# Seven of sixteen filter and matrix loads in the filter stage, and a z written contiguously

## The chip, the core and the metric

The kernel runs on one core of a Trainium2 chip. That core has a matrix engine (TensorE, in the profile PE, with its weight loads as PEld), a vector engine (VectorE, DVE), a scalar engine (ScalarE, ACT), GpSimd (POOL), which here does little more than issue transfers, and SyncE (SP), which only issues them. All transfers are carried by the core's 16 DMA engines, whoever issues them. The metric is the device time of one execution in microseconds.

## The reference

Two identical layers are applied to `x` of 2048 tokens by 576 features. Each layer adds a spectral block and then an MLP block to `x`:

```python
x = x + _A_ref(_layernorm(x), A_w_r, A_w_i)                   # spectral
x = x + _B_ref(_layernorm(x), B_w1, B_b1, B_w2, B_b2)         # MLP
# _A_ref: X = rfft2(x) over tokens and features; X = X * (w_r + 1j*w_i); irfft2, as bf16
# _B_ref: h = gelu(layernorm(x) @ w1 + b1), w1 is 576 x 4608;  h @ w2 + b2
```

The filter `w_r`, `w_i` has 2048 x 289 elements each. Inputs and output are bf16.

## The kernel before

The tokens are held in SBUF as 16 tiles of 128 x 576. The Fourier transforms are matrix products with constant matrices. The transform over the 2048 tokens is split into two factors, 16 and 128, with an exchange of partitions between them. So a layer goes through four stages.

**The filter stage** (`SpectralIn`, here meaning the forward transform up to the exchange) takes one tile after another. `fold` makes sum and difference of a tile's halves, `turn` transposes them on PE and copies the result out with ACT (`xT`), and `dft_d` multiplies by the feature-transform matrix into two PSUM banks: even frequencies (o = 0) in one bank, odd ones (o = 1) in the other. Each bank holds a real and an imaginary half (r) of 145 float32 values (j). At L423, one ACT instruction scales the 580 values by the tile's inverse deviation and writes them as bf16 to `z`, where the frequencies lie in natural order, so that even and odd alternate. `dft_v` multiplies by the 16-point matrix, and ACT or DVE copies the result to `y1`. `exchange` (L479) lets SP issue one transfer per tile that spreads it over 8 partitions of `vx`. In layer 0 the tiles come in one loop (`run_all`). In layer 1 they are worked in between the steps of layer 0's MLP, and only the last tile is on its own.

**The middle stage** (`middle`) needs all of `vx`. In a loop of 20 steps, step i does `dft_u(i)` on PE (matrix `c_f2`), an ACT copy, `weigh(i)` on DVE (products with the filter tiles `wks`), `join(i-1)` on DVE, and `idft_c(i-4)` on PE (matrix `i1s`) with a copy and another `exchange`, into `hx`. The slot numbers 0 to 15 go through four groups j = 0 to 3 of four slots each. Group j uses `f2` j, `wr` j, `wi` j and `i1` j, which makes sixteen loads in all, each 289 or 384 KB. Twelve filler matmuls (`keep_busy`) stand ahead of the loop.

**The back stage** (`SpectralOut`) needs all of `hx`, and 16 filler matmuls stand ahead of it. It adds the result to `x` and prepares the MLP's first input. Its matrices are `c_r1` and `c_gd`.

**The MLP** goes through four blocks of four tiles. `mlp_up` makes the hidden values of a block (GELU on ACT), and `mlp_down` the output, tile by tile. In layer 0, `fold_twice` and `turn_dma` prepare layer 1's spectral input as the tiles come out, and a second form of `dft_d` with the constant `c_fd2` transforms them. The w2 weights come in four parts during the first `mlp_up`, one for each of its first four groups of hidden chunks.

**The order of the work** is written by hand: every engine executes its instructions in program order. The loads that matter here go through `load` (L216), which puts the transfer on POOL's queue and, with an argument `behind`, lets POOL wait first for a marked instruction. In the filter stage, the list `first` (L882 to L892) is spread over the steps of `run_all`, each entry behind a tile's `xT` or `y1` copy. In the middle stage, `mid_loads` names for slot n the loads that wait for `join(n)`. In the MLP, the n-th entry of `w2_loads` waits for a GELU of group n.

Of the kernel before, what the change touches and what calls it, by code (L numbers as in the profile page):

```python
# [18 lines left out]
P = 128  # L19
# [3 lines left out]
KP = 2 * KH  # L23
# [100 lines left out]
def kernel(  # L124
# [15 lines left out]
    def const_ap(key):  # L140
        return nc.inline_tensor(hc[key], name=f"const_{key}").ap()
# [15 lines left out]
    def big_ps(shape, dtype=F32):  # L157
        return ps_big.tile(shape, dtype, tag="big", name=f"psb{uid()}")

    def sm_ps(shape, dtype=BF16):  # L160
        return ps_sm.tile(shape, dtype, tag="sm", name=f"pss{uid()}")
# [8 lines left out]
    def at(buf, shape, off=0):  # L170
        n = int(np.prod(shape[1:]))
        dims = "abcd"[: len(shape) - 1]
        return buf[0 : shape[0], off : off + n].rearrange(f"p ({' '.join(dims)}) -> p {' '.join(dims)}", **dict(zip(dims[1:], shape[2:])))
# [4 lines left out]
    c_fd2 = persist.tile([P, 4 * KH + 2 * KP], BF16, name="c_fd2")  # L178
    c_k1 = persist.tile([P, 3, P], BF16, name="c_k1")
    c_f2 = persist.tile([P, 16, 3, P], BF16, name="c_f2")  # L180
    c_r1 = persist.tile([P, 2, 256], BF16, name="c_r1")
    c_gd = persist.tile([P, 6, DH], BF16, name="c_gd")
# [3 lines left out]
    b1_rows = persist.tile([NFC, 128], BF16, name="b1_rows")  # L186
    b2_bc = persist.tile([P, D], BF16, name="b2_bc")
# [28 lines left out]
    def load(out, in_, behind=None):  # L216
        ins = nc.gpsimd.dma_start(out=out, in_=in_).ins
        if behind is not None:
            tc.add_manual_dep(ins, marks[behind].name, SYNC, reason="pace of the loads")
# [12 lines left out]
    def load_w(j, ri, behind=None):  # L232
        wv = (A_w_r, A_w_i)[ri].rearrange("(c e) k -> c e k", e=16)
        load(wks[j][:, :, ri, 0 : KP - 1], wv[:, j::4, :], behind)

    def load_i1(j, behind=None):
        load(i1s[j][:], i1_ap[:, j::4], behind)

    def load_f2(j, behind=None):
        load(c_f2[:, j::4], f2_ap[:, j::4], behind)  # L240

    def load_w1(ci, h):
        cols = slice(h * F_FF // 4, (h + 1) * F_FF // 4)
        return nc.sync.dma_start(out=w1_sb[:, ci, cols], in_=B_w1[ci * 128 : (ci + 1) * 128, cols]).ins

    def load_w1r(h):
        rest = B_w1[512:576, :].rearrange("d (j two p) -> d two j p", two=2, p=128)
        return nc.sync.dma_start(out=w1r_sb[64 * h : 64 * h + 64], in_=rest[:, h]).ins
# [4 lines left out]
    def place_w2():  # L253
        r_sb = shared_tile(BF16)
        w2_parts[:] = at(v_sb, [P, 8, D]), at(v_sb, [P, 8, D], 8 * D), at(r_sb, [P, 10, D]), at(r_sb, [P, 10, D], 10 * D)
# [5 lines left out]
    def load_w2(g, behind):  # L261
        rows = B_w2[w2_first[g] * 128 : w2_first[g + 1] * 128, :]
        load(w2_parts[g], rows.rearrange("(fc p) d -> p fc d", p=128), behind)
# [38 lines left out]
    class SpectralIn:  # L302
# [99 lines left out]
        def dft_d(self, t):  # L402
            pz = big_ps([P, 2, 512])
            if ("xT2", t) in self.st:
                xT = self.st.pop(("xT2", t))
                for o in range(2):
                    at_rest = 4 * KH + o * KP
                    nc.tensor.matmul(pz[:, o, 0:KP], lhsT=xT[:, 4, :], rhs=c_fd2[:, at_rest : at_rest + KP], start=True, stop=False)
                    for part in range(2):
                        g = FOLDS.index((o, part))  # L410
                        nc.tensor.matmul(
                            pz[:, o, part * KH : (part + 1) * KH], lhsT=xT[:, g, :], rhs=c_fd2[:, g * KH : (g + 1) * KH],
                            start=False, stop=(part == 1),
                        )
            else:
                xT = self.st.pop(("xT", t))
                for o in range(2):
                    for q, ci in enumerate(HALF_CHUNKS[o]):
                        nc.tensor.matmul(  # L419
                            pz[:, o, 0:KP], lhsT=xT[:, ci, :], rhs=c_fd[:, 3 * o + q, :], start=(q == 0), stop=(q == 2),  # L420
                        )
            z = work.tile([P, 2, KP], BF16, tag="z", bufs=3)
            nc.scalar.activation(  # L423
                out=z[:].rearrange("p r (j o) -> p r o j", o=2),
                in_=pz[:, :, 0:KP].rearrange("p o (r j) -> p r o j", r=2),
                func=ACT.Copy, scale=self.st.pop(("rs", t)),
            )
            self.st["z", t] = z
# [453 lines left out]
    first = [("x", 2), ("x", 3)]  # L882
# [1 line left out]
        first += [("f2", j), ("wr", j), ("wi", j), ("i1", j)]  # L884
    calls = {"x": load_x, "f2": load_f2, "i1": load_i1, "wr": lambda j, b: load_w(j, 0, b), "wi": lambda j, b: load_w(j, 1, b)}
    paced = {}
    for n, (kind, j) in enumerate(first[:-3]):
        i = 1 + 5 * n // 8
        if i <= NT:
            paced.setdefault(i, []).append(lambda kind=kind, j=j, i=i: calls[kind](j, ("turn", order[i - 1])))  # L890
        else:
            paced.setdefault(i, []).append(lambda kind=kind, j=j, i=i: calls[kind](j, ("y1", order[i - 4])))  # L892
# [6 lines left out]
    for li in range(N_LAYERS):  # L899
        last = li == N_LAYERS - 1  # L900
        out_loads = []
        mid_loads = {}
        if li == 0:
            mid_loads = {
                0: [lambda b: load_w(3, 0, b)],
                1: [lambda b: load_w(3, 1, b)],
                2: [lambda b: load_i1(3, b)],
                3: [lambda b: load(c_r1[:], const_ap("r1"), b)],
                4: [lambda b: load(c_gd[:], const_ap("gd"), b), lambda b: load(b1_rows[:], B_b1.rearrange("(fc p) -> fc p", p=128), b)],
                6: [lambda b: load(c_fd2[:], const_ap("fd2"), b)],  # L910
                5: [lambda b: load(b2_bc[:], B_b2.partition_broadcast(P), b)],
            }
        middle(vx, hx, wks, i1s, mid_loads)
        if li == 0:
            b1p = sm_ps([P, NFC])
            nc.tensor.transpose(b1p[:, :], b1_rows[:, :], ident[0:NFC, 0:NFC])
            nc.vector.tensor_copy(out=b1_sb[:], in_=b1p[:])
            out_loads = [lambda ci=ci: load_w1(ci, 0) for ci in range(4)] + [lambda h=h: load_w1r(h) for h in range(2)]
            out_loads += [lambda ci=ci, h=h: load_w1(ci, h) for h in range(1, 4) for ci in range(4)]
        prep = Prep(0, sqrt=True)  # L920
        SpectralOut(hx).run_all(prep, out_loads)
        place_w2()
        w2_loads = [lambda b, g=g: load_w2(g, b) for g in (0, 1, 2, 3)]
        if last:
            mlp(li, prep, None, w2_loads)
        else:
            vx, hx = at(b_sb, [P, 16, 2, KP]), at(v_sb, [P, 16, 2, KP])
            mlp(li, prep, SpectralIn(vx, sqrt=False), w2_loads)
            for j in range(4):
                b = ("y1", order[-1]) if j >= 2 else None  # L930
                load_w(j, 0, b)
                load_w(j, 1, b)
                load_i1(j, b)
# [27 lines left out]
```

## Time and profile before

| What | us |
|---|---|
| Median of 6 runs (747.42 to 751.56) | 747.67 |
| The profiled execution, its own time | 748.9 |
| Its span, first to last instruction | 747.1 |
| PE busy in the span | 725.4 |
| ACT busy | 314.8 |
| DVE busy | 273.0 |
| Layer 0: filter stage, to the middle's first matmul | 0 to 43.3 |
| Layer 0: middle stage, to the back stage's first matmul | 43.3 to 72.0 |
| Layer 1: middle stage, likewise | 405.4 to 432.5 |

The profile's page gives busy time per engine, the span in slices, the DMA queues, and the chain of work that ended last. Its further views list single instructions in order of time, waits by engine, and busy time in chosen stretches. In the latter, "DMA share" is the mean busy share of the 16 DMA engines and GB/s is what they moved. All times are counted from the start of the span.

### The profile page before, as it was taken

The numbers are of one execution on the slowest core, as the hardware profiler recorded it, in microseconds if no ns is written. First come the engines' busy times: TensorE is split into PE (matmuls) and PEld (weight loads), VectorE is DVE, ScalarE is ACT, GpSimd is POOL, SyncE is SP. The second block draws the span as 40 slices with busy tenths as digits, with TensorE's granted clock in tenths as the row PEclk, the third lists the DMA queues.
The fourth block names the chain that finished last, engine by engine and source line by source line (L and its number), as shares of the span: only waits on it lengthen the run. The fifth ranks groups of instructions, "written<-read, shape, count | busy, mean of one in ns | idle before, by whom it ended". The sixth has DMA issues, their size and how long they took to land. (4 is left out here: it accounts for less than half of the span.)

```text
span 747.1 us, 12382 instructions
## 1 busy us (share of the span) xinstructions
PE 725.4 (97%) x5000; PEld 454.7 (61%) x5038; DVE 273.0 (37%) x932; ACT 314.8 (42%) x530; POOL 61.6 (8%) x114
## 2 busy tenths in 40 slices
PE   7989999999999999999998999999999999999998
PEld 4655744784478447844785675467546744774476
DVE  6975870366036603630354859001400140010011
ACT  6955866115521452146324777530262045105600
POOL 4220012000100110000004000020100010000000
PEclk9999999999999999999999999999999999999999
DMA  8744925410121112210027401560001010200000
GB/s 261 233 127 148 283 66 181 120 44 26 44 56 50 26 44 54 52 35 0 18 44 223 126 17 36 171 150 25 35 11 44 17 44 0 45 17 8 1 17 17
DMA packets 49417, 54.45 MB, mean 73 GB/s; under 512 B 29892, under 2 KB 41104, under 8 KB 49360
## 3 DMA queue, kind: packets, MB, share of 16 engines
q1 hardware_dynamic: 41328, 23.99, 12.6%
q0 software_dynamic: 7600, 29.10, 12.3%
q8 instruction: 39, 0.64, 0.4%
q10 hardware_dynamic: 432, 0.58, 0.2%
q14 instruction: 18, 0.15, 0.1%
HBM read 29.34 MB, written 8.59 MB: 51 GB/s over the span
## 5 line engine op out<-in xcount | busy, mean ns | idle before, releaser
L806 PEld LDWEIGHTS <-h_sb 128*128 128x128 bf16 x2304 | 224.7, 98 | 58.8 <-issue 1.0
L761 PEld LDWEIGHTS <-w_sb 128*128 128x128 bf16 x1152 | 109.4, 98 | 142.5 <-issue 17.2
L274 DVE BATCH_NORM_STATS2 stats<-x_sb 128x6 f32<-128x288 bf16 x110 | 43.8, 440 | 1.1 <-DMA x_sb<-in_A_x_dram 1.1
L720 DVE TENSOR_SCALAR xn<-x_sb,mv,rs 128x576 bf16<-128x576 bf16 x24 | 9.4, 427 | 66.6 <-DMA quad_1769<-xn 27.6
L769 PEld LDWEIGHTS <-w1r_sb 64*128 64x128 bf16 x288 | 10.8, 94 | 24.5 <-issue 17.0
L802 DVE TENSOR_TENSOR xb<-x_sb,b_bc 128x576 f32<-128x576 bf16 x32 | 24.0, 749 | 0.0
L723 POOL COPY xn<-xn 128x64 bf16<-128x64 bf16 x24 | 6.4, 267 | 155.1 <-DVE xn L720 155.1
L527 PEld LDWEIGHTS <-h_sb 128*128 128x128 bf16 x128 | 12.1, 97 | 11.6 <-issue 6.2
L496 PEld LDWEIGHTS <-c_f_83 128*128 128x128 bf16 x128 | 12.3, 97 | 8.9 <-issue 3.3
L775 ACT ACTIVATE h_sb<-psb_5993,b_sb 128x512 bf16<-128x512 f32 x2 | 1.3, 684 | 37.9 <-PE psb_5993 L769 37.9
L775 ACT ACTIVATE h_sb<-psb_6591,b_sb 128x512 bf16<-128x512 f32 x2 | 1.3, 683 | 37.8 <-PE psb_6591 L769 37.8
L775 ACT ACTIVATE h_sb<-psb_7189,b_sb 128x512 bf16<-128x512 f32 x2 | 1.3, 683 | 37.8 <-PE psb_7189 L769 37.8
L829 DVE TENSOR_TENSOR x_sb<-psb_7429,xb 128x576 bf16<-128x576 f32 x1 | 0.8, 758 | 43.4 <-PE psb_7429 L806 43.4
L214 PEld LDWEIGHTS <-zeros 128*128 128x128 bf16 x95 | 9.4, 101 | 9.6 <-issue 1.7
L829 DVE TENSOR_TENSOR x_sb<-psb_4049,xb 128x576 bf16<-128x576 f32 x1 | 0.8, 758 | 39.5 <-PE psb_4049 L806 39.5
L352 DVE TENSOR_TENSOR xf<-ef 128x256 bf16<-128x256 f32 (+1 forms) x56 | 13.6, 305 | 0.5
L829 DVE TENSOR_TENSOR x_sb<-psb_6233,xb 128x576 bf16<-128x576 f32 x1 | 0.8, 759 | 33.6 <-PE psb_6233 L806 33.6
L829 DVE TENSOR_TENSOR x_sb<-psb_6831,xb 128x576 bf16<-128x576 f32 x1 | 0.8, 758 | 33.6 <-PE psb_6831 L806 33.6
L435 PEld LDWEIGHTS <-c_k_82 128*128 128x128 bf16 x120 | 11.3, 99 | 2.5
L419 PEld LDWEIGHTS <-xT 128*128 128x128 bf16 x96 | 9.9, 104 | 4.1 <-issue 1.1
L829 DVE TENSOR_TENSOR x_sb<-psb_3245,xb 128x576 bf16<-128x576 f32 x1 | 0.8, 758 | 28.7 <-PE psb_3245 L806 28.7
L678 ACT ACTIVATE h_sb<-x_sb 128x576 bf16<-128x576 bf16 x16 | 11.2, 699 | 0.1
(1367 smaller groups left out, 1500.1 us busy)
## 6 DMA issues: line engine op xcount, KB each, us to landing
w_sb<-in_B_w_dram SPq DMA_DIRECT2D x16, 288.0 KB
v_sb<-in_B_w_dram POOLq DMA_DIRECT2D x4, 1152.0 KB, 6.3
h_sb<-const_i POOLq DMA_DIRECT2D x8, 384.0 KB, 6.5
shared_1465<-in_B_w_dram POOLq DMA_DIRECT2D x2, 1440.0 KB, 7.7
shared_5390<-in_B_w_dram POOLq DMA_DIRECT2D x2, 1440.0 KB, 7.4
v_sb<-shared_113 SPq DMA_DIRECT2D x16, 145.0 KB
b_sb<-shared_691 SPq DMA_DIRECT2D x16, 145.0 KB
v_sb<-shared_4645 SPq DMA_DIRECT2D x16, 145.0 KB
```

What stands on the lines that cost most here:

```text
L214: nc.tensor.matmul(pw[:], lhsT=zeros[:], rhs=zeros[:, 0:1].to_broadcast([P, 512]), start=True, stop=True)
L274: nc.vector.bn_stats(out=stats[:, h, :], in_=x_sb[:, t, h * DH : (h + 1) * DH])
L352: nc.vector.tensor_tensor(out=xf[:, at0 : at0 + 2 * n].rearrange("p (g d) -> p g d", g=2), in0=ef[:, :, first : first + n], in1=ef[:, :, b ...
L419: nc.tensor.matmul(pz[:, o, 0:KP], lhsT=xT[:, ci, :], rhs=c_fd[:, 3 * o + q, :], start=(q == 0), stop=(q == 2),)
L435: nc.tensor.matmul(py[:, r, 0:KP], lhsT=c_k1[:, pl, :], rhs=z[:, ri], start=(q == 0), stop=(q == 1))
L496: nc.tensor.matmul(px[:, o, 0:KP], lhsT=c_f2[:, e, pl, :], rhs=vx[:, e, ri, :], start=(q == 0), stop=(q == 1))
L527: nc.tensor.matmul((ph, odd)[o][:, o, 0:KP], lhsT=i1[:, n % 4, pl, :], rhs=xp[:, ri, :], start=(q == 0), stop=(q == 1))
L678: nc.scalar.activation(out=at(h_sb, [P, D], 512 * 34), in_=x_sb[:, self.quad[i], :], func=(ACT.Copy, ACT.Square)[k], accum_out=self.s12[:, ...
L761: nc.tensor.matmul(acc[p][q], lhsT=w1_sb[:, ci, fc * 128 : (fc + 1) * 128], rhs=yT[:, ci, :], start=(first and ci == 0), stop=(not first a ...
L769: nc.tensor.matmul(acc[p][q], lhsT=w1r_sb[rows, p, :], rhs=yT[rows, 4, :], start=first, stop=not first)
L802: nc.vector.tensor_tensor(out=xb[:], in0=xr, in1=b2_bc[:].rearrange("p (h n) -> p h n", h=2), op=ALU.add)
L806: nc.tensor.matmul(po[:, h, 0:DH], lhsT=hts[fc][:, i * 128 : (i + 1) * 128], rhs=w2_chunk(fc)[:, h * DH : (h + 1) * DH], start=(fc == 0), ...
```

## The change

Three things change. First, the filter stage of layer 0 now issues the list `first` without its last seven entries, where it left out the last three. So `wr` 2, `wi` 2, `i1` 2 and `f2` 3 move into the middle stage, which then has seven of the sixteen loads, and its order is written anew. Second, `c_fd2` moves from the middle stage to a fifth entry of `w2_loads` in layer 0's MLP. Third, in `dft_d` the loop order of the ACT instruction is turned: for every j it handles both o, so that it writes `z` element after element and reads the two PSUM banks in turn, where it read each bank in runs of 145 and wrote every second element.

```diff
@@ dft_d @@
             nc.scalar.activation(
-                out=z[:].rearrange("p r (j o) -> p r o j", o=2),
-                in_=pz[:, :, 0:KP].rearrange("p o (r j) -> p r o j", r=2),
+                out=z[:].rearrange("p r (j o) -> p r j o", o=2),
+                in_=pz[:, :, 0:KP].rearrange("p o (r j) -> p r j o", r=2),
                 func=ACT.Copy, scale=self.st.pop(("rs", t)),
@@ paced loads of the filter stage @@
-    for n, (kind, j) in enumerate(first[:-3]):
+    for n, (kind, j) in enumerate(first[:-7]):
@@ loads of the middle stage, layer 0 @@
-                0: [lambda b: load_w(3, 0, b)],
-                1: [lambda b: load_w(3, 1, b)],
-                2: [lambda b: load_i1(3, b)],
-                3: [lambda b: load(c_r1[:], const_ap("r1"), b)],
-                4: [lambda b: load(c_gd[:], const_ap("gd"), b), lambda b: load(b1_rows[:], B_b1.rearrange("(fc p) -> fc p", p=128), b)],
-                6: [lambda b: load(c_fd2[:], const_ap("fd2"), b)],
-                5: [lambda b: load(b2_bc[:], B_b2.partition_broadcast(P), b)],
+                0: [lambda b: load_w(2, 0, b), lambda b: load_w(2, 1, b)],
+                1: [lambda b: load_f2(3, b)],
+                2: [lambda b: load_i1(2, b)],
+                3: [lambda b: load_w(3, 0, b), lambda b: load_w(3, 1, b)],
+                5: [lambda b: load_i1(3, b)],
+                6: [lambda b: load(c_r1[:], const_ap("r1"), b), lambda b: load(b1_rows[:], B_b1.rearrange("(fc p) -> fc p", p=128), b)],
+                7: [lambda b: load(c_gd[:], const_ap("gd"), b), lambda b: load(b2_bc[:], B_b2.partition_broadcast(P), b)],
@@ w2 loads @@
         w2_loads = [lambda b, g=g: load_w2(g, b) for g in (0, 1, 2, 3)]
+        if li == 0:
+            w2_loads.append(lambda b: load(c_fd2[:], const_ap("fd2"), b))
```

## The prediction

> **What bounds the kernel now.** I read the page first.
>
> ```profile
> span 747.1 us, 12382 instructions
> PE 725.4 (97%) x5000; PEld 454.7 (61%) x5038; DVE 273.0 (37%) x932; ACT 314.8 (42%) x530; POOL 61.6 (8%) x114
> ```
>
> PE is busy all along, but some of that is filler. The chain of work from 494 us on is MLP matmuls alone, so a delay in an earlier stage is not made good later. The change touches layer 0's filter stage (to 43.3) and middle stage (to 72.0). So next I read ACT's instructions in order of time:
>
> ```profile
> 23.32 0.92 ACT L423 ACTIVATE z<-psb_411,rs 128x580 bf16<-128x580 f32 x1
> 24.11 0.67 ACT L339 COPY xT<-pss_427 128x640 bf16<-128x640 bf16 x1
> 24.67 0.65 ACT L440 CAST shared_113<-psb_438 128x580 bf16<-128x580 f32 x1
> 25.20 0.94 ACT L423 ACTIVATE z<-psb_445,rs 128x580 bf16<-128x580 f32 x1
> 25.98 0.69 ACT L339 COPY xT<-pss_458 128x640 bf16<-128x640 bf16 x1
> 26.56 0.30 ACT L282 ACTIVATE sq<-mv_420,c_eps 128x2 f32<-128x2 f32 x1
> 27.16 0.93 ACT L423 ACTIVATE z<-psb_480,rs 128x580 bf16<-128x580 f32 x1 [0.30 <-PE psb_480 L419]
> 27.95 0.67 ACT L339 COPY xT<-pss_494 128x640 bf16<-128x640 bf16 x1
> ```
>
> Two tiles take 3.61 us (20.50 to 24.11) or 3.84 (24.11 to 27.95), 3.72 on average. From start to start a z costs 0.78, an xT 0.57, a y1 0.53, a root 0.30: 2 x 0.78 + 2 x 0.57 + 0.53 + 0.30 = 3.53 us for two tiles. ACT is the bound with 0.2 to spare. DVE is close behind: its shorter rounds, with no idle, take 3.6.
>
> For the middle stage I read busy time by stretches, and the waits of PE.
>
> ```profile
> core 0: us, PE busy (x) PEld busy (x) DVE busy (x) ACT busy (x) POOL busy (x), PEclk, DMA share, GB/s
> 49.00:59.00 10.00, 9.27 (x64) 6.08 (x64) 10.00 (x34) 8.80 (x16) 3.45 (x6) 1.00 0.82 233
> 59.00:69.00 10.00, 9.89 (x61) 5.77 (x61) 6.57 (x22) 5.18 (x9) 0.00 (x0) 1.00 0.54 183
> ```
> ```profile
> PE psb_705 L496 <- DMA v_sb<-shared_113: 1.4, 1, 1.4
> PE pss_1036 L567 <- DMA b_sb<-shared_691: 1.2, 1, 1.2
> ```
>
> The second wait is the one to look at: the back stage starts at 72.0 because the last exchange comes late, although filler covers PE until 70.8. SP issued it at 66.6, so it took 5.3 us. In layer 1, whose middle has hardly any loads, the same transfer is issued at 428.7 and all traffic is over by 432.0: 3.3 us, and PE never waits. So layer 0's exchanges are held up by the loads beside them, and the rows show how: after the loads, from 59 to 69, the traffic stays at a flat 183 GB/s and a share of 0.54, a backlog being worked off.
>
> [...]the trace has 920, while the plain copy of the same 580 values (642) and of 290 (401) agree with the slope.[...] No row of before reads PSUM element by element from two banks.
>
> **z, part by part.** Removed is the write at every second element. A GELU with one pointer, 512 values, takes 684: 257 fixed. With 257 + 580 x 0.833 = 740 as the best case, the gain is at most 180 ns. Added is a read that changes bank with every element[...]. If that costs a second cycle per element, z takes 257 + 580 x 1.667 = 1,224 ns, 300 more. I take this end: [...]already the milder stride on the write side goes with 180 ns lost.
>
> At 1,224, two tiles cost ACT 3.53 + 0.60 = 4.13, with a little dependency idle 4.2, against 3.72: +0.48. The loop has some 6.5 such pairs at full pace (15.7 to 36.2): +3.1. The first tiles and the last z, on the way to the final exchange, add 0.3 each: +3.7. At 740, ACT falls to 3.17 and DVE's 3.58 takes over: -0.14 x 6.5 - 0.16 = -1.0. The 15 z of the MLP cost nothing either way: ACT idles 5.8 us before most of them, and dft_v stands 24 matmuls (2.9 us) behind dft_d; without that cover they would cost 15 x 0.3 = 4.5.
>
> **Loads out of the filter stage.** 289 + 289 + 384 + 384 = 1,346 KB leave it. No compute instruction waits there for anything but x, so only the last exchange can gain: issued 39.7, waited for until 43.2, 3.5 us against 3.3 undisturbed: -0.2. POOL's issues (0.75 each) delay nobody.
>
> **Loads into the middle.** There 1,346 come and c_fd2's 290 goes: +1,056 KB.[...] The shares from 47 to 71 add up to 14.6 us of all engines. The 16 exchanges (16 x 145 KB = 2.38 MB) at 183 GB/s need 13.0 us on their engines, 7.0 of the whole set. That leaves 7.5 us per engine for the 1,965 KB loaded, 3.84 ns per KB. Check: 13.0 + 7.5 = 20.5 of the 21.5 us from 49 to 70.5: these engines hardly rest. Then 1,056 x 3.84 = +4.06 us until the last exchange lands: about 76.0 where it was 72.0. As PE already waits, all of it shows: +4.0.
>
> The moved loads also come later for their users. By the same price, and the pace of before (57% of the engine's time goes to loads: `i1` 3 landed 6.7 us after its issue at 49.4), `f2` 3 lands at 55.6 (needed 56.4), `i1` 2 at 58.1 (57.2), `wi` 3 at 61.8 (59.5), `i1` 3 at 64.3 (62.1). So PE or DVE stalls by some 2.3 us in all: DVE at weigh(12), with join and idft_c behind it. That moves the end of the filler from 70.8 to 73.1, still before 76.0, so it is contained in the 4.0 and not added. c_r1 and c_gd land by 68, before the back stage.
>
> **c_fd2 in the MLP.** POOL's fifth load waits for the GELU at 131.6, and behind it in POOL's queue stand the copies and stores for the next block's input, issued from 127.3 on. They start 5.5 us later; then DVE's fourth norm (135.1, behind which the first output tile's add at 142 waits) comes near 138 to 140. SP's transpose (138.3) moves to about 143; its result is wanted near 171. c_fd2 lands near 139, first used at 155.4. Cost 0; with that cover gone at most 5.5.
>
> **Sum.** +3.7 - 0.2 + 4.0 = +7.5. The profiled execution, 748.9 with its span of 747.1, would become 756.4; it lies 1.2 above the median, so 747.67 + 7.5 = 755.2.
>
> **Rivals.**
> (1) z gets faster (740 to 900 ns), loads as above: -1.0 - 0.2 + 4.0 = +2.8, 750.5.[...]
> (2) The loads hide: backlog is worked off in the middle's own time[...]. With slow z: +3.7 - 0.2 = +3.5, 751.2. Against it: the flat 0.54 until 69.
> (3) Not slower: z at 740 with loads hidden, -1.2, 746.5. Decisive is the last exchange's landing: if it comes before the filler's end at 70.8, the loads cost nothing, and PE even saves its 1.2 us wait: -2.4, 745.3.[...]
>
> **Chances and range.** Likeliest case 0.50; rival 1 0.28; rival 2 0.12; rival 3 0.10. Two executions of this kernel can't be told apart below 0.3%, 2.2 us. Rival 3 lies almost wholly inside that, a fifth of it beyond; a quarter of rival 1 falls inside and a little of rival 2: faster 0.02, same 0.18, slower 0.80. Range: below, rival 1 with loads at 3 us, 749.3; above, loads at 5.5[...] and z at 1,300: 758.5. The likeliest case alone: 753 to 758.
>
> **What would show it.** z's duration at L423 (1.2 or 0.74) and the distance between tiles in the filter stage (4.2 or 3.6 for two); PE's wait at L567 for the exchange growing from 1.2 towards 4, with DMA shares of 0.8 until some 66 us; a stall of DVE at L507 or L508, or PE at L527, for h_sb. The prediction is wrong if z stays near 0.92 or falls, or if L567 starts by 73 plus what the filter stage lost.

## The result and the profile after

| | before | changed |
|---|---|---|
| Median, us | 748.16 (20 runs, 746.63 to 751.56) | 751.24 (10 runs, 748.87 to 751.61) |
| Profiled execution, its own time / its span | 748.9 / 747.1 | 750.09 / 748.3 |
| Filter stage's end: the middle's first matmul (L496) | 43.27 | 42.24 |
| Back stage's first matmul (L567) | 71.99 | 73.02 |
| Length of the middle, between these two | 28.72 | 30.78 |
| From L567 to the first MLP's first matmul (L761) | 25.43 | 25.44 |

The changed kernel is slower by the ratio 1.0032 (95% interval 1.0020 to 1.0045), some 3 us. The forecast was 755.2; the change costs less than half of what was summed. (After the change nine of the sixteen filter and matrix loads stand in the filter stage and seven in the middle, not the other way round, as the title could be read.) The page after, first its span and part 1, busy time by engine:

```profile
span 748.3 us, 12381 instructions
PE 724.9 (97%) x5000; PEld 454.5 (61%) x5038; DVE 273.2 (37%) x932; ACT 310.5 (41%) x530; POOL 61.6 (8%) x114
```

ACT has lost 4.3 us of busy time, DVE and PE next to nothing. So `z` has become cheaper, where the forecast had made it dearer. ACT in order of time in the changed kernel, columns start, duration, engine, line, and in brackets the idle time before and what ended it:

```profile
26.23 0.74 ACT L423 ACTIVATE z<-psb_476,rs 128x580 bf16<-128x580 f32 x1 [0.30 <-PE psb_476 L419]
26.87 0.68 ACT L339 COPY xT<-pss_490 128x640 bf16<-128x640 bf16 x1
27.44 0.66 ACT L440 CAST shared_113<-psb_501 128x580 bf16<-128x580 f32 x1
27.98 0.77 ACT L423 ACTIVATE z<-psb_508,rs 128x580 bf16<-128x580 f32 x1
...
30.47 0.69 ACT L339 COPY xT<-pss_557 128x640 bf16<-128x640 bf16 x1
```

A `z` takes 0.74 to 0.77 us instead of 0.92. Two tiles take 3.60 us (26.87 to 30.47), and ACT now has idle time of its own, 0.30 ahead of every second `z`. DVE has none in these rounds, and its work on two tiles starts again after 3.60 us:

```profile
26.70 0.81 DVE L274 BATCH_NORM_STATS2 stats<-x_sb 128x6 f32<-128x288 bf16 x2
...
30.30 0.81 DVE L274 BATCH_NORM_STATS2 stats<-x_sb 128x6 f32<-128x288 bf16 x2
```

It is the new bound, at the 3.6 that the prediction's best case had for it. The middle starts 1.03 us earlier.

Then the loads. Busy time by stretches in the changed kernel, the last two columns being the DMA share and GB/s:

```profile
core 0: us, PE busy (x) PEld busy (x) DVE busy (x) ACT busy (x) POOL busy (x), PEclk, DMA share, GB/s
49.00:59.00 10.00, 9.22 (x64) 6.12 (x64) 10.00 (x33) 8.80 (x16) 4.46 (x8) 1.00 0.98 280
59.00:69.00 10.00, 8.35 (x53) 4.79 (x52) 5.63 (x19) 4.25 (x8) 0.00 (x0) 1.00 0.54 189
69.00:71.00 2.00, 2.00 (x11) 0.88 (x9) 0.00 (x0) 0.00 (x0) 0.00 (x0) 1.00 0.51 175
71.00:73.00 2.00, 0.34 (x2) 0.01 (x1) 0.00 (x0) 0.00 (x0) 0.00 (x0) 1.00 0.09 31
```

Where before had a share of 0.82 from 49 to 59, it is 0.98 now. The flat tail at 0.54, exchanges alone (8.6 of the 16 DMA engines), lasts until 70.5 and not until 69. The waits in the same stretch (in total, times, longest):

```profile
ACT shared_687 L535 <- DMA b_sb<-shared_687: 2.5, 3, 1.7
...
PE pss_1035 L567 <- DMA b_sb<-shared_687: 1.7, 1, 1.7
PE psb_975 L527 <- DVE shared_687 L514: 1.6, 1, 1.6
DVE shared_687 L533 <- DMA b_sb<-shared_687: 1.5, 1, 1.5
```

The second line is the wait that the forecast followed, 1.69 us where it was 1.22. The first and the last are new, and the forecast has nothing of them: the copies into the eight `h` buffers (L528, slot n mod 8) wait for the exchange that last read from the same buffer. The third, PE's wait at L527, follows from them: `join` (L514) stands behind DVE's wait in DVE's order. None of these waits is for a load.

### The profile page after: what moved, and what is told of

Read it like the earlier page. It is cut to its first block, busy times and chain, and to the rows that moved or that the text cites. A ratio compares the mean times of both kernels' runs of the same rounds, so it can differ in the third digit from the quotient of the medians.

```text
span 748.3 us, 12381 instructions
## 1 busy us (share of the span) xinstructions
PE 724.9 (97%) x5000; PEld 454.5 (61%) x5038; DVE 273.2 (37%) x932; ACT 310.5 (41%) x530; POOL 61.6 (8%) x114
## 5 line engine op out<-in xcount | busy, mean ns | idle before, releaser
L761 PEld LDWEIGHTS <-w_sb 128*128 128x128 bf16 x1152 | 109.4, 98 | 142.4 <-issue 17.2
L527 PEld LDWEIGHTS <-h_sb 128*128 128x128 bf16 x128 | 12.1, 97 | 13.2 <-issue 7.8
L496 PEld LDWEIGHTS <-c_f_83 128*128 128x128 bf16 x128 | 12.3, 97 | 9.2 <-issue 3.6
L829 DVE TENSOR_TENSOR x_sb<-psb_7429,xb 128x576 bf16<-128x576 f32 x1 | 0.8, 758 | 43.4 <-PE psb_7429 L806 43.4
L829 DVE TENSOR_TENSOR x_sb<-psb_4049,xb 128x576 bf16<-128x576 f32 x1 | 0.8, 758 | 39.5 <-PE psb_4049 L806 39.5
L829 DVE TENSOR_TENSOR x_sb<-psb_6831,xb 128x576 bf16<-128x576 f32 x1 | 0.8, 759 | 33.6 <-PE psb_6831 L806 33.6
L829 DVE TENSOR_TENSOR x_sb<-psb_6233,xb 128x576 bf16<-128x576 f32 x1 | 0.8, 758 | 33.6 <-PE psb_6233 L806 33.6
L829 DVE TENSOR_TENSOR x_sb<-psb_3245,xb 128x576 bf16<-128x576 f32 x1 | 0.8, 759 | 28.7 <-PE psb_3245 L806 28.7
```

What stands on the lines that cost most here:

```text
L496: nc.tensor.matmul(px[:, o, 0:KP], lhsT=c_f2[:, e, pl, :], rhs=vx[:, e, ri, :], start=(q == 0), stop=(q == 1))
L527: nc.tensor.matmul((ph, odd)[o][:, o, 0:KP], lhsT=i1[:, n % 4, pl, :], rhs=xp[:, ri, :], start=(q == 0), stop=(q == 1))
L761: nc.tensor.matmul(acc[p][q], lhsT=w1_sb[:, ci, fc * 128 : (fc + 1) * 128], rhs=yT[:, ci, :], start=(first and ci == 0), stop=(not first a ...
```

## The experiments

Two reasons had to be tried: that `z`'s saving comes from the write side while the read from two banks is free, and that the loads slow the exchanges on the 16 DMA engines, whose share went from 0.82 to 0.98 (theory A). Its rival B: the ring of eight `h` buffers, whose waits are new, delays the last exchange. What the runs brought up beside these was tried next.

### Each part alone

`e1_z_only` is the kernel before with the two lines of L424 and L425 alone. `e2_loads_only` is the changed kernel without them:

```diff
-                out=z[:].rearrange("p r (j o) -> p r j o", o=2),
-                in_=pz[:, :, 0:KP].rearrange("p o (r j) -> p r j o", r=2),
+                out=z[:].rearrange("p r (j o) -> p r o j", o=2),
+                in_=pz[:, :, 0:KP].rearrange("p o (r j) -> p r o j", r=2),
```

`e3_z_and_fd2` is the kernel before with the new `z`, and with `c_fd2` moved to the MLP; none of the other loads is moved.

> The kernel before with the turned loop order of z alone. z takes 744 ns as in the kernel after (920 before). Theory A (z shortens ACT's rounds in layer 0's filter stage until DVE bounds them): the middle stage's first matmul comes 1.0 us earlier (42.2 where it was 43.3), the middle stage keeps its 28.7 us, the time falls by 1.0 us (0.13%). Rival B (the filter stage's gain is given back, because the exchanges it sends sooner queue behind the same loads): first matmul of the middle within 0.3 us of 43.3, no change of the time.

> The kernel after with z's loop order of before, so the moved loads alone. Theory A (the moved loads cost what the middle stage of the kernel after shows): filter stage as before or 0.2 us shorter, middle stage 30.8 us where it was 28.7, time +2.0 us (0.27%), and the change of the kernel after is the sum of this run and of z alone. Rival B (the price of 3.84 ns per KB of the prediction holds and the faster filter stage hid part of it in the kernel after): middle stage 32 to 33 us, time +3.5 to +4.0 us.

> The kernel before with the turned loop order of z and with c_fd2 loaded in the first MLP block; the other loads stay where they were, so the middle stage carries 290 KB less than before. Theory A (bytes in the middle stage hold up its last exchange): the back stage's wait for it shrinks from 1.2 us to between 0.1 and 0.7, so the time falls by 1.0 for z and 0.5 to 1.1 more: -1.5 to -2.1 us (0.2 to 0.28%). Rival B (a load that late in the middle stage costs nothing): -1.0 us, wait still 1.2.

Beside one median of before, 748.02 (36 runs), the three took:

| | median, us | ratio to before, 95% | L496 | L567 |
|---|---|---|---|---|
| `z` alone | 747.84 | 0.9996 (0.9987 to 1.0004) | 41.85 | 69.41 |
| loads alone | 750.92 | 1.0042 (1.0027 to 1.0058) | 42.80 | 73.20 |
| `z` and `c_fd2` | 747.17 | 0.9984 (0.9976 to 0.9992) | 41.93 | 69.27 |

So the loads are the whole loss. The expectations were met in part. With `z` alone L496 comes early, so the gain of the filter stage is not given back there, but the median falls by 0.2 us and not by 1.0, and the middle takes 27.56 us, not 28.7. With the loads alone the middle takes 30.40 us, as theory A had it and not 32 to 33; the time rises by 2.9 us, more than its 2.0. `z` and `c_fd2` together gain 0.85 us, not 1.5 to 2.1, though the wait at L567 is gone.

The two useful parts together, without the moved loads, are faster than both kernels. That `c_fd2` costs nothing in the MLP is seen here too.

Loads alone had one thing more in its trace. Busy time by stretches of that kernel, where the third column from the right is the granted PE clock (PEclk):

```profile
71.00:73.00 2.00, 0.17 (x1) 0.00 (x0) 0.00 (x0) 0.00 (x0) 0.00 (x0) 1.00 0.19 64
73.00:75.00 2.00, 1.80 (x22) 1.30 (x23) 0.00 (x0) 0.67 (x2) 0.00 (x0) 0.65 0.00 0
75.00:77.00 2.00, 2.00 (x10) 1.35 (x9) 0.00 (x0) 1.08 (x2) 0.00 (x0) 0.50 0.61 191
77.00:79.00 2.00, 2.00 (x26) 1.53 (x24) 1.67 (x4) 1.08 (x3) 0.00 (x0) 1.00 1.04 359
```

After a PE wait of 2.03 us at L567 the clock reads 0.65 from 73 to 75, 0.50 from 75 to 77, and is back at 1.00 from 77 on. In this profile the way from L567 to L761 takes 26.84 us and not 25.43: 1.4 us more.

### Twelve h buffers

`e4_after_ring12` is the changed kernel with a ring of twelve:

```diff
-            h = at(r_sb, [P, 2, KP], 592 * (2 + 9 + n % 8))
+            k = n % 12
+            h = at(r_sb, [P, 2, KP], 592 * (11 + k)) if k < 8 else at(h_sb, [P, 2, KP], 4 * GROUP + 592 * (k - 8))
```

> The kernel after with twelve buffers for the middle stage's results ahead of their exchange, not eight. In the kernel after, copies of DVE and ACT wait 1.5 and 1.7 us near 61 us for an exchange to free its buffer. Theory A (the exchanges' DMA engines are the bound, the buffer wait is only where it shows first): these waits go, the last exchange is issued some 1.5 us earlier and lands at the same time, the back stage starts within 0.4 us of 73.0 with a wait of about 3 us, time as the kernel after. Rival B (the buffer wait itself costs the time): the back stage starts 1.5 us earlier, time 1.5 us below the kernel after.

The waits for the ring are gone and the filler is done earlier, at 70.1, but L567 starts at 73.09. What PE no longer waits in the loop, it waits there:

```profile
73.09 0.60 PE L568 MATMUL pss<-c_r,b_sb 128*128 128x256 bf16 x4 [3.00 <-DMA b_sb<-shared]
```

(One line was added, so L567 is L568 here.) B falls, and theory A is left. SP issues the last exchange 23.9 us after L496, where it was 25.0 in the changed kernel, and yet L567 starts 30.50 us after L496 against 30.78: of 1.1 us that the exchange is issued sooner, 0.3 is left where PE waits for it. The kernel took 752.01, ratio 1.0048 (1.0032 to 1.0064). That isn't faster, and here too the clock falls after the wait:

```profile
73.00:75.00 2.00, 1.91 (x23) 1.42 (x24) 0.00 (x0) 0.97 (x2) 0.00 (x0) 0.70 0.00 0
75.00:77.00 2.00, 2.00 (x11) 1.28 (x10) 0.00 (x0) 0.78 (x2) 0.00 (x0) 0.50 0.76 232
```

From L567 to L761 it takes 26.88 us.

### z in four forms

`e5_z_forms` is the kernel before with four forms of the `z` instruction, by the tile's number:

```diff
+            ways = (
+                ("p r (j o) -> p r o j", "p o (r j) -> p r o j"),
+                ("p r (j o) -> p r j o", "p o (r j) -> p r j o"),
+                ("p r (o j) -> p r o j", "p o (r j) -> p r o j"),
+                ("p r (o j) -> p r j o", "p o (r j) -> p r j o"),
+            )
+            to, frm = ways[t // 4]
```

> The kernel before, with z's copy in four forms, four tiles each: (1) output written at every second element, input read in runs of one bank (before's form); (2) output written in one run, input read from the two banks in turn (the change's form); (3) output and input both in runs (z's frequencies come out in another order, so what follows computes with permuted frequencies; only durations are read from it); (4) output written at every second element or in another scattered order, input read from the two banks in turn (again permuted). Theory that the change's result suggests: only the output's order costs, the change of bank costs nothing. Then (1) 0.92, (2) 0.74, (3) 0.74, (4) 0.92 us. The prediction's reason, softened: the change of bank costs something, but less than the scattered write did; then (3) comes out shorter than (2), at 0.65 to 0.72, and (4) longer than (1), at 1.0 or more.

The tiles' order in the loop goes through the quarters in turn, so four consecutive `z` show all four, from form 1 to form 4. What follows does not undo the other order of frequencies in forms 3 and 4, so this kernel's output is not the reference's. ACT in order of time:

```profile
19.28 0.91 ACT L430 ACTIVATE z<-psb,rs 128x580 bf16<-128x580 f32 x1
...
21.74 0.74 ACT L430 ACTIVATE z<-psb,rs 128x580 bf16<-128x580 f32 x1 [0.82 <-PE psb L419]
...
23.98 0.74 ACT L430 ACTIVATE z<-psb,rs 128x580 bf16<-128x580 f32 x1
...
25.51 2.86 ACT L430 ACTIVATE z<-psb,rs 128x580 bf16<-128x580 f32 x1
```

Forms 2 and 3 both take 0.74: the change of bank with every element costs nothing here, and the 0.17 by which form 1 is longer (0.91) is the price of writing every second element. So the prediction's reason falls even when softened, as form 3 is no shorter than form 2. Form 4 writes to two places 290 bytes apart in turn. The first theory had 0.92 for it, the second only "1.0 or more"; it takes 2.86, which is 2.1 us over form 2 with the very same reads, (2,860 - 740) / 580 = 3.7 ns more per element. In layer 0, three tiles have it at this line (the sixteenth tile is copied in halves elsewhere), and 3 x 2.1 = 6.3 us fit the late start of the middle, 49.38 against 42.87 on average in the profiles with the old `z`. That is most of the 8 us by which this kernel, at 756.0, is longer.

Form 1, which writes every second element, pays 0.3 ns per element (0.17 / 580) over the form that writes one after the other, form 4 the 3.7 ns above. Why such writes take longer is not shown by these runs.

### More filler against the fall of the clock

Theory C: an idle PE of 2 us and more lowers the clock, in many executions of the changed kernel too. It is tried with more work that nobody needs, ahead of the first block's back stage. `e6_after_fill24` is the changed kernel, `e7_ring12_fill28` that of twelve buffers (with 28):

```diff
-            keep_busy(16)
+            keep_busy(24 if u2r_turn[0] == 0 else 16)
```

> The changed kernel, with 24 filler matmuls in place of 16 ahead of the first block's back stage; that is 8 x 0.214 = 1.7 us more of work that nobody needs, about the 1.69 us that PE waits there in the changed kernel's profile. The filler would end near 72.9, the last exchange lands near 72.2 to 73. Theory C (an idle PE of nearly 2 us lowers the granted clock in many executions of the changed kernel, and costs them some 1.4 us): clock 1.00 in the back stage, and faster than the changed kernel by 0.5 to 1.4 us, ratio to the kernel before 1.0013 to 1.0025. Rival (the clock has no part in the changed kernel's own time, filler is only filler): same as the changed kernel or later by up to 0.5 us, ratio 1.0032 to 1.0040.

> The changed kernel with twelve h buffers, and 28 filler matmuls in place of 16 (12 x 0.214 = 2.57 us more). With 16 the kernel of twelve buffers waited 3.00 us at the back stage's start, its clock fell to half for some 3 us after it, and it took 752.01. Theory C: the wait shrinks to about 0.4 us, the clock stays at 1.00, from the start of the back stage to the first block's MLP goes back from 62.9 to 61.5 us, and the median falls by about 1.4, to 750.6, ratio 1.003. Rival (the clock fell for another reason[...]): it falls again, 752.0 and ratio 1.0048 stay.

Before took 747.91 (52 runs) beside them. `e6`: 750.14, ratio 1.0025 (1.0016 to 1.0034), L567 at 72.87 after a wait of 0.29. `e7`: 750.09, ratio 1.0028 (1.0020 to 1.0037), L567 at 72.51 after a wait of 0.58. Busy time by stretches of `e7`:

```profile
73.00:75.00 2.00, 1.90 (x28) 1.60 (x28) 0.00 (x0) 1.75 (x3) 0.00 (x0) 1.00 0.20 23
75.00:77.00 2.00, 2.00 (x27) 1.57 (x27) 1.76 (x4) 1.18 (x3) 0.00 (x0) 1.00 0.94 303
```

With 2.6 us more filler, the kernel of twelve buffers is 1.9 us faster than without (752.01 to 750.09), 1.5 by the ratios. The two intervals just overlap, but four of the five times without it lie above all eighteen with it, the clock in the profile stays at 1.00, and from L567 to L761 it takes 25.44 us and not 26.88: the rival fell there. For the changed kernel the step is 1.1 (751.24 to 750.14) or, by the ratios, 0.5; it is in the direction expected, but the two intervals overlap. Of the changed kernel's ten timed executions, the two at a mean clock of 1.000 took 748.87 and 749.77, the eight at 0.995 to 0.998 took 750.27 to 751.61, which fits theory C; but with `z` alone, executions at 0.995 (747.43, 748.5) are no longer than some at 1.000 (749.03), and of the 52 executions of before the 23 with a mean clock below 0.999 have the median 747.86, the other 29 747.94. So a mean clock is no proof. For the kernel of twelve buffers the runs agree with theory C (clock 0.50 with a wait of 3.00 us, 1.00 with 0.58), for the changed kernel itself it is only likely.

The clock fell to 0.50 after 2.03 us (`e2`) and 3.00 us (`e4`) without a matmul. In two other executions it stayed at 1.00 after waits about as long: 2.03 us in a second profile of the changed kernel (`e11`) and 2.00 us in `e12`, both below. So no length of wait that decides it can be read from these runs.

### Less filler

`e8_z_fd2_fill12` is the kernel of `e3` with `keep_busy(12 if u2r_turn[0] == 0 else 16)`.

> The kernel before with the new z and c_fd2 in the MLP (no other load moved, b1, gd and b2 keep their places), and 12 filler matmuls in place of 16 ahead of the first block's back stage. With 16 the last exchange had landed by 68.4, and the back stage started at 69.27, when the filler was over. If the filler is the bound there, 4 x 0.214 = 0.86 us less filler start the back stage at 68.4, and the median is 746.3 to 746.7 (ratio 0.997 to 0.998, against 0.9984 with 16). If the exchange takes over at once, nothing changes: 747.2, 0.9984; and if PE then waits long enough to lose clock, it is slower, 748 and more.

It took 746.91, ratio 0.9988 (0.9979 to 0.9997); L567 starts at 68.50 with a wait of 0.80 for the exchange. That is 0.8 us earlier than in `e3`'s profile, but so is L496 (41.08, there 41.93): the middle takes 27.42 us against 27.34, and a wait stands where four filler matmuls stood. So the exchange took over at once, as the second case of the expectation has it, and the filler hid it almost exactly. The two ratios can't be told apart. Both `e3` and this kernel beat the kernel before and the changed one.

### How far one profile stands for a kernel

In the profile of `z` alone, with the loads of before, PE did not wait for the last exchange at all. So the kernel before was profiled twice more and the changed one once more.

> The kernel before, profiled once more, to learn how far its one profile stands for it. In that profile the last exchange was issued at 66.6, landed near 71.5 and PE waited 1.2 us for it; with only z changed, and the same loads, it landed at 68.3 without a wait. If this comes from z, it shows again here: wait near 1.2, landing about 28 us after the middle's first matmul (L496). If single executions differ by it, the wait comes out anywhere from 0 to 1.2, the landing 26.5 to 28 us after, and the two kernels' loads are then no proof of engines that never rest.

> The kernel before, a third profile, for the same question: the wait at L567 near 1.2 us in every execution, or anywhere from 0 to 1.2.

> The changed kernel, profiled once more. If the wait at L567 with its late loads is a property of the kernel, it is 1.5 to 2.1 us again, the landing about 30 us after L496; where it reaches 2 us, the granted clock of the back stage falls to some 0.5 for 2 to 4 us. If it is chance, 0 to 1.7.

PE's first matmul of the back stage, in the second and third profile of before:

```profile
69.80 0.60 PE L567 MATMUL pss<-c_r,b_sb 128*128 128x256 bf16 x4
```
```profile
71.53 0.60 PE L567 MATMUL pss<-c_r,b_sb 128*128 128x256 bf16 x4 [1.00 <-DMA b_sb<-shared]
```

and in the second of the changed kernel:

```profile
74.16 0.60 PE L567 MATMUL pss<-c_r,b_sb 128*128 128x256 bf16 x4 [2.03 <-DMA b_sb<-shared]
```

The three executions of before took 748.9, 748.54 and 750.12, those of the changed kernel 750.09 and 752.4. So the wait of 1.2 us from which the prediction started is not in every execution: in one of three, with the same loads, the exchanges come in time.

A part of this lies in how the exchanges end. Read in quarters of a microsecond, the DMA share falls from 0.54 to 0.07, close to what one engine of sixteen would give (1/16 = 0.06), and stays near that for about a microsecond in the two profiles of before that wait (70.25 to 71.25 and 69.75 to 70.75). In the one without a wait it is over by 69.0, with no such tail; the second profile of the changed kernel has 0.07 from 72.0 to 73.25. So by this estimate a single engine ends the last exchange late in some executions; which one and why is not shown.

### One more dose

`e12_after_fd2mid` is the changed kernel with `c_fd2`'s 290 KB in the middle again, behind its other loads:

```diff
+                8: [lambda b: load(c_fd2[:], const_ap("fd2"), b)],
...
-        if li == 0:
-            w2_loads.append(lambda b: load(c_fd2[:], const_ap("fd2"), b))
```

> The changed kernel, with c_fd2's 290 KB loaded in the middle again (at n = 8, behind all other loads) and not in the MLP: one more dose of load beside the exchanges. By the measured price of some 3.2 ns per KB the back stage starts 0.9 us later, by the prediction's 3.84 it starts 1.1 us later, about 74 us, with a PE wait near 2.7 us, and as that wait is beyond 2 us the clock falls too: ratio to the kernel before 1.0045 to 1.006 (752.0 to 752.5). If the exchanges' engines had room left at that point[...], nothing changes: L567 at 73, 1.0032. If c_fd2's place in the MLP had cost something, it is faster than the changed kernel.

It took 751.96, ratio 1.0050 (1.0031 to 1.0068), with L567 at 74.01 after a wait of 2.00; the clock stayed at 1.00 in the profile, against the expectation. The middle took 31.87 us. With the other profiles this makes a series, all with 16 filler matmuls and eight buffers:

| loads in the middle, against before | middle (L496 to L567), us | mean |
|---|---|---|
| -290 KB (`e3`) | 27.34 | 27.34, ended by the filler |
| as before (before three times, `e1`) | 28.72, 27.44, 28.49, 27.56 | 28.05 |
| +1,056 KB (changed twice, `e2`) | 30.78, 31.41, 30.40 | 30.86 |
| +1,346 KB (`e12`) | 31.87 | 31.87 |

From the second row to the third it is 2.81 / 1,056 = 2.7 ns per KB; from the third to the fourth, 1.01 / 290 = 3.5, on one profile. Two of the second row, 27.44 and 27.56, were also ended by the filler, but only just: the exchanges' traffic is over by 69.0 and 68.75 there, some 0.7 to 0.8 us before L567, the distance at which PE also starts where it does wait. With 290 KB less the exchange itself ended the middle in `e8`, after 27.42 us. The rows differ in the order of the loads as well as in KB, and no run separates the two.

## Why the prediction was wrong

The sum was +3.7 (`z`), -0.2 (the filter stage's exchange), +4.0 (loads). The runs put these in its place:

- **"At 1,224, two tiles cost ACT 4.13": the step that failed.** `z` takes 744, the prediction's own best case of 740. The 0.833 ns per element of that best case is in the trace of before: copies of 580 and of 290 values take 642 and 401 ns, (642 - 401) / 290 = 0.83. That a read from two banks in turn pays this twice, hence 1,224, was the author's assumption, which no trace of before could show. It was taken because the stride on the write side went with a loss. That loss was itself the answer: the two forms differ in both sides, and the one price that the trace showed belonged to the write, as `e5` tells. The read in turn costs nothing (0.74 in forms 2 and 3). Over nine profiles with the new `z`, L496 starts at 41.95 on average, over four with the old one at 42.87: -0.9, where +3.7 was taken and -1.0 worked out for the best case, with DVE as the next bound, as it is.
- **"3.84 ns per KB", "these engines hardly rest": mis-sized.** The direction is right: more load in the middle makes it longer (28.05 us as before, 30.86 with 1,056 KB more), the ring of buffers is not the cause (`e4`), and the wait at L567 is for the last exchange. That loads and exchanges compete for the very same few engines was the author's assumption: exchanges alone show a share of 0.54, 8.6 of 16 engines, but no view tells which engines carry what. But the term measured 2.8 us in the length of the middle, not 4.06. The sum of the engine's time was made from 49 on, in a profile where the exchanges end late, and took all of the room as used. In the changed kernel the share in the first ten microseconds goes from 0.82 to 0.98, so part of the added traffic seems to fit into what had been free; and one profile of before in three shows no wait at all. What came on top of nearly full engines cost near the price that was taken, 3.5 in the last step of the series, on one profile.
- **-0.2 for the filter stage's own exchange.** Not seen: the wait at L496 lies between 1.3 and 1.9 us with the loads in either place. It was below what single profiles tell.
- **The moved loads late for their users, 2.3 us of stall.** No such wait came, as the loads landed 3 to 4 us earlier than estimated (the last of them, `i1` 3, at 60.0 and not at 64.3). The stall that did come, 1.5 us of DVE and 2.5 of ACT, was for the ring of eight buffers, which the prediction overlooked. As it said of its own stall, this is contained in the delay of the last exchange and not added to it: with twelve buffers nothing is gained.
- **`c_fd2` in the MLP, cost 0.** Right. POOL issues it at 133.63, and the copies behind it in its queue start at 134.18 where they started at 127.27. The first output tile's add (L829) starts at 143.51 where it started at 142.47, and these 1.04 us are the delay with which the MLP began (98.46, before 97.42).
- **What the sum lacked: the clock.** In two of the four profiles where PE waited 2 us or more at L567 (`e2`, `e4`), the clock fell to 0.50, and the way from L567 to L761 was 1.4 us longer each time (26.84 and 26.88, against 25.43). The prediction counted a wait at its length only.

Remade, the sum is -0.9 for `z`, +2.8 for the loads and some +0.5 to +1.1 for the clock, an estimate from the step to `e6`, which is only likely: +2.4 to +3.0, against 3.1 between the medians. The medians of the two parts alone, -0.2 and +2.9 with the clock in it, give +2.7. Rival 1 (faster `z`, loads that show in full, +2.8, 750.5) named the right outcome in both parts, a shorter `z` and loads that show, and the time came out beside it (751.24), the smaller price of the loads and the fall of the clock cancelling out. (The ends of the prediction's range, summed again from its own terms, come to about 749.5 and 758; nothing above rests on them.)

Two things stay open. `z` alone brings the middle forward by about 0.9 us in the profiles, but its median is only 0.2 below before (interval -1.0 to +0.3). And the time from L567 in layer 0 to L567 in layer 1 comes out between 360.5 and 362.3 us in three executions of the kernel before, with a part of it, up to 1.0, in layer 1's own middle; no run tells why. A single pair of profiles, as the one of the first table, can't be subtracted to better than that.

## What to carry to other kernels

A strided access has two sides: before pricing a change that turns one into the other, look for the rows that differ in one side only, and where there are none, keep the two prices at equal weight (here the write cost 0.17 us, the read nothing). A price per KB taken from the backlog of a shared transfer path can overstate what more traffic costs (here 3.84 ns per KB was taken and 2.7 came) while the engines have room (a share of 0.82 in the first ten microseconds of the middle's loads); see first, in more than one profile, how much of the time they were full. And an idle matrix engine may cost more than its wait: in two of four profiles here a wait of 2 us or more was followed by a halved clock, 1.4 us in the stage behind it.

## What was not expected of the hardware

- ACT reading float32 from two PSUM banks in turn, element by element: 0.74 us for 580 values, the same as in runs of 145 (`e5`, forms 2 and 3).
- ACT writing bf16 at every second element: +0.17 us for 580 (0.91 against 0.74, form 1). Writing in turn to two places 290 bytes apart: +2.1 us (2.86, form 4).
- The clock of PE at 0.50 after waits of 2.03 (`e2`) and 3.00 us (`e4`), and at 1.00 after 1.69 (changed), 2.00 (`e12`) and another 2.03 (`e11`).
